# Linear attention and a two-layer feed-forward: one hand-fixed order of 3436 operations replaced by another

## The chip, the cores and the metric

The kernel runs on one core of a Trainium2 chip. The metric is the device time of one execution in microseconds (us): the median of three runs is 794.76 us before the change, with 792.8 and 801.1 as the lowest and the highest. The core has a matmul engine (PE, with its weight loads shown apart as PEld), three engines for elementwise work (DVE, ACT, POOL) and the queue engine SP, which issues most DMAs; ACT issues some. Each engine takes its instructions strictly in the order in which the program lists them, and an instruction that must wait holds up all that stand behind it on its engine.

## The reference

```
q_s = exp(q - max(q over d));  q_s /= sum(q_s over d) + 1e-9
k_s = exp(k - max(k over s));  k_s /= sum(k_s over s) + 1e-9
kv  = einsum("bhsd,bhse->bhde", k_s, v)
x   = einsum("bhsd,bhde->bhse", q_s, kv)     # 8 batches, 8 heads, 576 rows, 64 wide
x   -> 4608 tokens x 512
h   = x @ w_in                               # 512 x 2048
g   = h if h >= 1; 0 if h <= -1; else (h + 1)^2 / 4
out = g @ w_out                              # 2048 x 512
```

## The kernel before, in words

The 4608 tokens are cut into 9 chunks of 512. Per chunk the attention is done for pairs of heads: softmax of q and k on DVE, ACT and POOL, the products k^T v (`kv`, line 1288, for the first chunk line 1044) and q times kv (`x`, line 918) on PE. All large matmuls work on pairs of rounded numbers: a value is stored as a high part (a CAST on ACT) and the rest (a subtraction on DVE or POOL), and each product is three matmuls, high by low, high by high and low by high. The weights arrive as 64-bit numbers (`st`, loads of 512 KB) and are taken apart in the first chunk: ACT scales (`sg`, line 579), DVE shifts and joins (lines 584 and 587), ACT rounds to the high part (line 610), POOL subtracts (line 614). The parts of w_in go to a buffer in DRAM (`b`) and are fetched again (`w`, line 652) for later chunks.

Chunks 0 to 2 are computed plainly. For a block f of 128 of the 2048 hidden units, the first layer fills one PSUM bank (`h`, line 1499, 12 matmuls of 512 columns), ACT and POOL or ACT build the squared ramp (`r`, lines 1669 and 1673 or 1675), DVE clips it into the bank (line 1679), ACT rounds it (`g`, line 1721), DVE subtracts (line 1725), and the second layer adds it to four output banks (`o`, line 1736). The bank of block f is free for block f + 3 once the subtraction of line 1725 is done. Chunks 3 to 8 go in pairs by a scheme of seven block products in place of eight: the first layer with `hA`, `hb`, `hC` (line 1563), its sums on DVE (line 1587), the same ramp (now into rooms called B11, B12, B21, B22), sums of these rooms (line 1841), their rounding on ACT (line 1855) and the subtraction on DVE or POOL (line 1859), then the second layer (`yA`, `yB`, `yC`, line 1879). The bank of the last `hA` of a pair is also the first `yB` bank.

The maxima of k that the softmax subtracts travel through DRAM: DVE finds and turns them (`kmax`, `mt`, lines 1245 and 1251), SP stores them (`mk`, line 1255) and loads them back to all 128 partitions (`m`, line 1263), and DVE subtracts them from k (line 1272).

Nothing is scheduled at run time. A planner builds 3436 operations with their dependences; the tuple `SEQUENCE` holds the numbers of all of them in the order in which they are emitted, and each engine gets its share of that order. An operation that can be done by two engines has a second way, and the tuple `SECOND` lists the operations that take it (427 of them): most are subtractions and sums that DVE does in place of POOL, some are copies that DVE does in place of ACT. `Plan.settle` applies both tuples; buffers that rotate are assigned in the order of the sequence too.

Of the kernel before, what the change touches and what calls it, by code (L numbers as in the profile page):

```python
# [99 lines left out]
class Ring:  # L100
# [31 lines left out]
    1, 43, 20, 0, 19, 44, 95, 62, 11, 2, 46, 63, 12, 102, 30, 13, 21, 31, 47, 86, 14, 87, 128,  # L132
    88, 3, 89, 45, 15, 90, 4, 22, 91, 16, 92, 32, 54, 93, 64, 94, 23, 33, 55, 17, 330, 34, 96,
    25, 331, 18, 65, 35, 6, 56, 109, 24, 97, 26, 36, 57, 7, 37, 98, 27, 58, 49, 99, 5, 59, 8,
    66, 48, 9, 104, 100, 103, 28, 73, 50, 10, 105, 51, 74, 29, 68, 106, 67, 38, 107, 75, 69, 76,
    52, 70, 130, 154, 129, 77, 135, 60, 41, 131, 78, 39, 71, 61, 53, 132, 40, 79, 72, 133, 332,
    115, 80, 333, 81, 180, 42, 334, 310, 111, 134, 141, 156, 155, 101, 335, 82, 142, 336, 312,
    157, 84, 83, 167, 110, 337, 85, 168, 158, 112, 338, 169, 159, 137, 113, 170, 136, 116, 114,
    171, 138, 117, 339, 182, 143, 181, 172, 161, 311, 139, 118, 183, 318, 140, 193, 119, 173,
    194, 184, 340, 187, 120, 144, 185, 206, 174, 121, 195, 175, 196, 122, 232, 145, 123, 219,  # L140
    162, 163, 146, 220, 197, 164, 124, 165, 147, 126, 341, 166, 148, 221, 342, 149, 222, 189,
    213, 188, 127, 313, 343, 322, 198, 152, 190, 321, 178, 344, 191, 208, 125, 207, 314, 192,
    223, 209, 151, 224, 199, 153, 345, 239, 210, 234, 316, 150, 315, 200, 211, 176, 214, 201,
    177, 215, 346, 258, 179, 216, 203, 225, 233, 317, 347, 245, 217, 319, 235, 226, 246, 479,
    218, 227, 236, 205, 241, 240, 247, 237, 265, 242, 248, 260, 202, 284, 249, 323, 228, 259,
    243, 229, 261, 250, 231, 244, 262, 251, 271, 320, 252, 263, 291, 272, 724, 253, 273, 324,
    267, 266, 274, 349, 204, 268, 275, 286, 254, 269, 276, 285, 230, 270, 287, 297, 277, 298,
    288, 293, 356, 292, 299, 289, 325, 294, 255, 348, 295, 300, 375, 278, 296, 326, 301, 279,
    302, 382, 256, 327, 458, 329, 460, 328, 282, 351, 350, 478, 257, 352, 362, 303, 353, 363,
    358, 357, 354, 364, 304, 359, 365, 305, 360, 406, 281, 377, 290, 376, 361, 283, 378, 388,  # L150
    384, 383, 459, 379, 389, 385, 469, 366, 390, 380, 413, 461, 367, 309, 462, 386, 480, 391,
    463, 466, 368, 401, 392, 464, 481, 432, 369, 393, 280, 402, 370, 482, 308, 387, 403, 307,
    483, 408, 419, 420, 407, 470, 485, 394, 409, 395, 484, 415, 410, 414, 416, 396, 487, 465,
    404, 439, 417, 373, 411, 486, 433, 306, 421, 422, 471, 371, 434, 445, 446, 447, 423, 435,
    436, 374, 440, 437, 424, 468, 448, 418, 372, 467, 472, 400, 397, 497, 398, 488, 441, 442,
    449, 473, 425, 443, 426, 489, 399, 474, 427, 490, 510, 511, 450, 451, 512, 381, 491, 186,
    452, 475, 499, 430, 429, 444, 513, 428, 492, 493, 477, 494, 523, 504, 476, 498, 453, 500,
    501, 431, 506, 609, 505, 1306, 507, 496, 514, 607, 457, 502, 525, 524, 526, 530, 456, 531,
    527, 238, 554, 515, 528, 454, 536, 1394, 455, 508, 537, 538, 495, 509, 532, 533, 405, 627,
    539, 516, 517, 608, 549, 518, 519, 520, 534, 628, 567, 556, 629, 550, 552, 553, 568, 521,  # L160
    540, 541, 503, 569, 685, 705, 551, 561, 630, 535, 555, 610, 611, 557, 558, 542, 543, 706,
    707, 631, 544, 570, 562, 571, 563, 564, 559, 708, 580, 545, 632, 581, 572, 686, 944, 565,
    586, 573, 612, 587, 582, 588, 613, 589, 574, 522, 590, 575, 546, 633, 438, 634, 615, 745,
    614, 583, 584, 746, 566, 747, 687, 616, 709, 617, 264, 725, 591, 547, 529, 748, 592, 593,
    646, 710, 648, 594, 711, 647, 548, 712, 692, 635, 693, 694, 585, 688, 689, 691, 713, 690,
    721, 649, 695, 578, 718, 637, 636, 1172, 638, 722, 597, 639, 560, 577, 749, 696, 719, 731,
    618, 750, 732, 697, 108, 576, 733, 771, 734, 579, 596, 941, 698, 595, 699, 946, 620, 778,
    650, 723, 779, 943, 601, 598, 599, 780, 781, 651, 737, 735, 619, 600, 700, 758, 736, 621,
    738, 741, 759, 652, 772, 640, 701, 751, 702, 641, 642, 643, 760, 742, 773, 782, 720, 603,
    703, 752, 753, 602, 605, 774, 761, 762, 657, 763, 622, 714, 715, 645, 791, 644, 775, 716,  # L170
    623, 777, 704, 864, 792, 783, 764, 740, 765, 654, 810, 667, 793, 653, 784, 794, 776, 807,
    766, 666, 804, 862, 756, 624, 658, 668, 669, 817, 795, 769, 743, 805, 818, 717, 656, 670,
    730, 671, 757, 808, 673, 819, 1487, 820, 822, 770, 739, 809, 785, 754, 726, 831, 832, 786,
    844, 845, 672, 796, 821, 833, 863, 865, 744, 755, 797, 798, 626, 660, 866, 834, 835, 1073,
    836, 846, 847, 811, 901, 674, 659, 661, 867, 823, 873, 940, 848, 799, 902, 675, 625, 655,
    903, 767, 768, 908, 909, 868, 827, 789, 837, 870, 788, 662, 824, 676, 677, 678, 1303, 874,
    787, 910, 606, 663, 679, 828, 911, 849, 850, 838, 904, 800, 1130, 905, 806, 869, 826, 1076,
    680, 907, 790, 802, 664, 934, 935, 851, 803, 665, 825, 912, 839, 842, 160, 852, 682, 684,
    857, 829, 681, 921, 860, 906, 861, 913, 914, 922, 872, 801, 915, 923, 916, 875, 843, 871,
    1301, 683, 882, 936, 937, 924, 947, 858, 876, 925, 840, 987, 926, 830, 948, 938, 961, 949,  # L180
    962, 963, 841, 974, 951, 927, 855, 975, 950, 883, 964, 212, 953, 952, 954, 1483, 877, 976,
    957, 988, 928, 1132, 989, 859, 878, 1026, 814, 977, 958, 939, 853, 856, 978, 884, 929, 1028,
    604, 995, 990, 959, 979, 980, 885, 919, 854, 920, 965, 917, 886, 887, 918, 991, 992, 1397,
    879, 1065, 1066, 993, 955, 994, 930, 996, 997, 960, 998, 889, 966, 981, 1176, 1173, 1392,
    967, 1027, 1035, 956, 931, 968, 969, 891, 982, 999, 1067, 1029, 1079, 933, 1030, 1008, 888,
    1000, 1001, 1009, 1068, 1010, 1011, 890, 1038, 1071, 1170, 932, 1080, 1002, 892, 971, 984,
    1069, 1081, 1072, 893, 894, 972, 1082, 1003, 1083, 895, 896, 1093, 1085, 1094, 1095, 1032,
    973, 986, 1084, 1037, 1096, 898, 1131, 1106, 1133, 1086, 1070, 881, 1031, 970, 1034, 1074,
    1087, 1012, 1013, 1033, 1089, 1014, 900, 1097, 1005, 880, 1098, 897, 899, 729, 983, 1107,
    1108, 1109, 1090, 1091, 1004, 1015, 1016, 985, 1021, 1046, 1047, 816, 1110, 1099, 1177,  # L190
    1006, 1036, 1040, 1178, 1017, 1141, 1100, 1088, 1179, 1180, 1048, 1049, 1101, 1134, 1022,
    1023, 1217, 1183, 1092, 1218, 1039, 1184, 1007, 1186, 1050, 1181, 1051, 1024, 1018, 1185,
    1020, 1111, 1103, 1112, 1052, 1053, 1041, 1138, 1113, 1105, 1054, 1102, 1055, 1019, 1169,
    1042, 1056, 1057, 1139, 1114, 1182, 1204, 1078, 1205, 1225, 1116, 1115, 1058, 1206, 1219,
    1187, 1059, 1135, 1226, 1136, 1060, 1061, 1188, 1137, 1119, 1025, 1043, 727, 1063, 1044,
    1104, 1117, 1207, 1150, 1045, 1127, 1142, 1227, 1143, 1228, 1208, 1220, 1221, 1222, 1209,
    1129, 1191, 1192, 1193, 1194, 1579, 1140, 1189, 1210, 1062, 1128, 1121, 1229, 1230, 1145,
    1118, 1144, 1211, 1299, 1231, 1064, 1658, 1195, 1196, 1146, 1122, 1151, 1212, 1197, 1305,
    1232, 1190, 1120, 1152, 1223, 1198, 1300, 1321, 1293, 1294, 1322, 1323, 1256, 1125, 1254,
    1199, 1324, 1325, 1224, 1307, 1126, 1238, 1296, 355, 1147, 1201, 1577, 1297, 1298, 1239,  # L200
    1233, 1123, 1655, 1153, 1326, 1327, 1203, 1154, 1155, 1156, 1240, 1200, 1157, 1213, 1334,
    1255, 412, 1241, 1242, 1148, 1347, 1348, 1308, 1309, 1158, 1216, 1257, 1258, 1259, 1243,
    1244, 1335, 1214, 1237, 1160, 1159, 1161, 1310, 1260, 1202, 1215, 1328, 1236, 1149, 1162,
    1245, 1163, 1164, 1336, 1246, 1265, 1311, 1262, 1313, 1165, 1337, 1266, 1338, 1171, 1312,
# [2059 lines left out]
```

## Time and profile before

| | us |
|---|---|
| median of 3 runs (lowest, highest) | 794.76 (792.8, 801.1) |
| span of the profiled execution, first to last instruction | 791.4 |
| PE busy with matmuls | 780.8 |
| DVE busy | 610.0 |
| ACT busy | 469.3 |
| POOL busy | 395.5 |

The span is that of one profiled execution; what lies around it (start and end of the program) isn't in the trace, and the profiled execution has no time of its own beside the span. The median of the runs is 3.4 us above the span. Busy times are sums of instruction durations without overlap; matmuls are pipelined, so that two neighbours overlap and their number times their duration is more than the busy time.

### The profile page before, as it was taken

The numbers are of one execution on the slowest core, as the hardware profiler recorded it, in microseconds if no ns is written. First come the engines' busy times: TensorE is split into PE (matmuls) and PEld (weight loads), VectorE is DVE, ScalarE is ACT, GpSimd is POOL, SyncE is SP. The second block draws the span as 40 slices with busy tenths as digits, with TensorE's granted clock in tenths as the row PEclk, the third lists the DMA queues.
The fourth block names the chain that finished last, engine by engine and source line by source line (L and its number), as shares of the span: only waits on it lengthen the run. The fifth ranks groups of instructions, "written<-read, shape, count | busy, mean of one in ns | idle before, by whom it ended". The sixth has DMA issues, their size and how long they took to land.

```text
span 791.4 us, 12315 instructions
## 1 busy us (share of the span) xinstructions
PE 780.8 (99%) x4136; PEld 630.1 (80%) x4136; DVE 610.0 (77%) x1035; ACT 469.3 (59%) x868; POOL 395.5 (50%) x343
## 2 busy tenths in 40 slices
PE   8999999999999999999999999999999999999998
PEld 6777878877777778877778888777778888888886
DVE  7988887667788888788789886887797846669843
ACT  7868775555565665655675664665756625555560
POOL 5766466745456556356653465346405632344250
PEclk9999999999999999999999999999999999999999
DMA  8988998999799787987777767756656746667663
GB/s 315 294 269 287 298 338 276 319 311 363 263 336 320 258 304 233 348 302 251 228 221 256 233 245 249 248 185 212 192 180 222 245 163 207 204 187 231 211 207 136
DMA packets 76462, 200.74 MB, mean 254 GB/s; under 512 B 8688, under 2 KB 16880, under 8 KB 76400
## 3 DMA queue, kind: packets, MB, share of 16 engines
q1 hardware_dynamic: 64160, 174.43, 66.0%
q10 hardware_dynamic: 12240, 25.54, 10.1%
q8 instruction: 33, 0.54, 0.3%
q14 instruction: 29, 0.24, 0.1%
HBM read 159.02 MB, written 40.91 MB: 253 GB/s over the span
## 4 chain that ended last, share of the span: by engine, by line
PE 86%; DVE 4%; DMA 4%; ACT 3%; issue 1%; POOL 1%; SPq 0%; POOLq 0%; DVEq 0%; ACTq 0%
PE hA L1563 16%; PE yA L1879 16%; PE o L1736 13%; PE h L1499 12%; PE yC L1879 8%; PE hC L1563 8%; PE yB L1879 4%; PE hb L1563 4%; PE kv L1288 2%; PE x L918 2%; DMA st<-in_w 1%; DMA kt<-in_kt 1%; DVE st L587 1%; DMA w<-b 1%; DMA m<-mk 1%
## 5 line engine op out<-in xcount | busy, mean ns | idle before, releaser
L1855 ACT CAST y<-B 128x512 fp32r<-128x512 f32 x160 | 99.0, 621 | 79.3 <-PE yA L1879 34.9
L1563 PE MATMUL hA<-x,w 128*128 128x512 f32 x576 | 142.5, 390 | 0.0
L1859 POOL TENSOR_TENSOR y<-B,y 128x512 fp32r<-128x512 f32 x55 | 74.3, 1356 | 113.7 <-ACT y L1855 104.1
L1563 PEld LDWEIGHTS hA<-x,w 128*128 128x128 f32 x576 | 107.8, 188 | 23.2 <-DVE sn_P L481 0.8
L1879 PE MATMUL yA<-y,w_y 128*128 128x512 f32 x528 | 124.5, 390 | 0.0
L1736 PE MATMUL o<-wh,g 128*128 128x512 f32 x384 | 118.6, 390 | 0.0
L1879 PEld LDWEIGHTS yA<-y,w_y 128*128 128x128 f32 x528 | 98.9, 188 | 21.4 <-ACT y L1855 0.8
L1499 PE MATMUL h<-x,w 128*128 128x512 f32 x432 | 109.5, 392 | 0.8 <-DVE g L1725 0.8
L1859 DVE TENSOR_TENSOR y<-B,y 128x512 fp32r<-128x512 f32 x105 | 83.7, 802 | 32.5 <-ACT y L1855 31.8
L1675 POOL TENSOR_TENSOR r<-r 128x512 f32<-128x512 f32 x46 | 50.5, 1102 | 94.6 <-ACT r L1669 89.5
L1499 PEld LDWEIGHTS h<-x,w 128*128 128x128 f32 x432 | 80.4, 188 | 19.1 <-DVE g L1725 1.8
L1736 PEld LDWEIGHTS o<-wh,g 128*128 128x128 f32 x384 | 72.1, 188 | 15.2 <-DVE g L1725 0.6
L1736 PE MATMUL o<-wl,g 128*128 128x512 f32 x192 | 76.0, 396 | 0.6 <-ACT g L1721 0.6
L1563 PE MATMUL hC<-x,w 128*128 128x512 f32 x288 | 73.3, 392 | 0.0
L1879 PE MATMUL yC<-y,w_y 128*128 128x512 f32 x288 | 66.7, 389 | 0.0
L1673 ACT ACTIVATE r<-r 128x512 f32<-128x512 f32 x98 | 61.3, 630 | 5.7 <-DMA r<-wh 2.4
L1563 PEld LDWEIGHTS hC<-x,w 128*128 128x128 f32 x288 | 53.7, 188 | 11.8 <-ACT sn_P L479 0.3
L1879 PEld LDWEIGHTS yC<-y,w_y 128*128 128x128 f32 x288 | 54.1, 188 | 11.2
L1841 DVE TENSOR_TENSOR B<-B,B 128x512 f32<-128x512 f32 x72 | 51.7, 735 | 0.6
L1396 POOL TENSOR_TENSOR q<-q,qmb 128x512 f32<-128x512 f32 x32 | 36.0, 1138 | 30.2 <-DVE qmb L1388 21.7
L1396 POOL TENSOR_TENSOR q<-q,qzb 128x512 f32<-128x512 f32 x32 | 35.4, 1118 | 26.5 <-DVE qzb L1418 17.8
L1736 PEld LDWEIGHTS o<-wl,g 128*128 128x128 f32 x192 | 36.0, 188 | 11.8 <-issue 3.5
(156 smaller groups left out, 1404.5 us busy)
## 6 DMA issues: line engine op xcount, KB each, us to landing
w_y<-r SPq DMA_DIRECT2D x84, 512.0 KB, 4.1
w<-b SPq DMA_DIRECT2D x50, 512.0 KB, 5.5
w<-s SPq DMA_DIRECT2D x48, 512.0 KB, 4.6
st<-in_w SPq DMA_DIRECT2D x32, 512.0 KB, 6.2
s<-w_s SPq DMA_DIRECT2D x16, 512.0 KB, 6.1
r<-w_o SPq DMA_DIRECT2D x32, 256.0 KB, 4.8
v<-in_v ACTq DMA_DIRECT2D x20, 325.0 KB, 4.7
k<-in_k ACTq DMA_DIRECT2D x20, 320.0 KB, 5.1
```

The lines of the kernel that those rows point to most:

```text
L918: nc.tensor.matmul(flat(r)[cols, p0:p1], kvt[rows, g % NKV, pr, :], q[pr]["tq"].rearrange("p j t -> p (j t)")[rows, p0:p1], start=True, st ...
L1288: nc.tensor.matmul(kv[d, i, :], t[pr]["k"][:, j, d], t[pr]["v"][:, j, e * (D + 1) : (e + 1) * (D + 1)], start=(j == 0), stop=(j == KJ - 1) ...
L1396: nc.gpsimd.tensor_tensor(qf, qf, at, alu)
L1499: nc.tensor.matmul(t["h"], lhs, rhs, start=(turn == 0 and i == 0), stop=(turn == NPAIR - 1 and i == 2),)
L1563: nc.tensor.matmul(banks[b]["h"], lhs, rhs, start=(begins and not kk and not m), stop=(ends and kk == 1 and m == 2), skip_group_check=True,)
L1673: nc.scalar.activation(t["r"], t["r"], AF.Square)
L1675: nc.gpsimd.tensor_tensor(t["r"], t["r"], t["r"], ALU.mult)
L1736: nc.tensor.matmul(outs[c, j], lhs[:, s], rhs, start=(begins and i == 0), stop=(closes and i == 2),)
L1841: eng.tensor_tensor(gr[p, to], gr[p, a], gr[p, b], alu)
L1855: nc.scalar.copy(t["gh"], gr[p, PART_ROOM[part]])
L1859: eng.tensor_tensor(t["gl"], gr[p, PART_ROOM[part]], f32(t["gh"]), ALU.subtract)
L1879: nc.tensor.matmul(banks[b, i], lhs, rhs, start=(begins and not m), stop=(ends and m == 2), skip_group_check=True,)
```

## The change

Only the two tuples change. `SEQUENCE` has the same 3436 numbers in another order: an operation stands on average 8.5 places from where it stood, the largest moves are 165 places ahead and 176 back, and the 200 places from 1800 on are the same. `SECOND` has 440 numbers in place of 427. DVE has 1053 instructions in place of 1035, ACT (its DMA issues included) 947 in place of 949, POOL 323 in place of 339; PE has the same matmuls. The longer tuple moves every later line down by one, so that line 1679 of before is line 1680 of the changed kernel.

```
 SEQUENCE = (
-    1, 43, 20, 0, 19, 44, 95, 62, 11, 2, 46, 63, 12, 102, 30, 13, 21, 31, 47, 86, 14, 87, 128,
...
 SECOND = (
-    10, 27, 29, 51, 61, 70, 72, 146, 172, 198, 276, 328, 329, 393, 450, 476, 491, 605, 625, 626,
...
```

**SP, first chunk, about 40 us into the program.** The names: `k_1_1` is a load of k of chunk 1, `st5_1` and `st7_0` are weight loads, `mk1_0` the store of the maxima, `m2_1_0` their load back. Before:

```order
L1235 DMA v_1_1_693<-in_v 128x650
L1235 DMA k_1_1_700<-in_k 128x640
L572 DMA st5_1_730<-in_w 128x1024
L1255 DMA mk1_0_189<-mt_1_0_715 4x32 x2
L572 DMA st7_0_754<-in_w 128x1024
L1263 DMA m2_1_0_766<-mk1_0_189 128x256
L1235 DMA v_1_0_775<-in_v 128x650
```

Now:

```order
L573 DMA st4_1_690<-in_w 128x1024
L1236 DMA k_1_0_721<-in_k 128x640
L1256 DMA mk1_0_189<-mt_1_0_708 4x32 x2
L1236 DMA v_1_1_738<-in_v 128x650
L573 DMA st5_1_743<-in_w 128x1024
L1264 DMA m2_1_0_760<-mk1_0_189 128x256
L573 DMA st7_0_765<-in_w 128x1024
```

The store of the maxima stood behind the weight load st5_1 and now stands ahead of it; the load back stood behind the weight load st7_0 and now stands ahead of it, and st5_1 is behind one more load of v.

**DVE, chunk 1, about 180 us into the program.** The names: `sw_6`, `ss_6`, `w_s_6`, `os_5` and `w_o_5` are sums of weights for the later chunks, `h_1_10` is the bank of block 10 of chunk 1 that line 1679 clips, `kmax`, `qa`, `qmo`, `qmb`, `z` and `rz` belong to the softmax. Before:

```order
L684 TENSOR_TENSOR sw_6_2177<-w_1_13_2171 128x512
L1679 SCALAR_TENSOR_TENSOR h_1_11_2141<-h_1_11_2141,r_1_11_2215 128x512
L1370 TENSOR_REDUCE qa_3_0_2217<-q_3_1_2154 128x16
L1388 TENSOR_TENSOR qmb_3_0_2251<-qa_3_0_2217,qmo_3_0_2246 128x32
L698 TENSOR_TENSOR ss_6_2256<-ss_6_2256,sw_6_2177 128x256
L1299 TENSOR_SCALAR z_3_0_2260<-kv_3_0_2180 128x2
L1301 RECIPROCAL rz_3_0_2262<-z_3_0_2260 128x2
L736 TENSOR_TENSOR w_s_6_0_2264<-ss_6_2256,w_s_6_0_2264 128x2x256
L698 TENSOR_TENSOR ss_6_2256<-sw_6_2177 128x256
L698 TENSOR_TENSOR ss_6_2256<-sw_6_2177,ss_6_2256 128x256
L1679 SCALAR_TENSOR_TENSOR h_1_10_2126<-h_1_10_2126,r_1_10_2241 128x512
L1245 TENSOR_REDUCE kmax_94<-kt_4_0_2201 128x1
```

Now:

```order
L1680 SCALAR_TENSOR_TENSOR h_1_9_2026<-h_1_9_2026,r_1_9_2157 128x512
L941 TENSOR_TENSOR x10_2106<-x_2_0_0_2057,x10_2106 128x512
L787 TENSOR_TENSOR os_5_2115<-ow_5_2054 128x256
L1680 SCALAR_TENSOR_TENSOR h_1_10_2131<-h_1_10_2131,r_1_10_2180 128x512
L685 TENSOR_TENSOR sw_6_2217<-w_1_12_2183 128x512
L832 TENSOR_TENSOR w_o_5_1_2189<-os_5_2115,w_o_5_1_2189 128x2x256
L1726 TENSOR_TENSOR g_1_9_2226<-h_1_9_2026,g_1_9_2226 128x512
L1300 TENSOR_SCALAR z_3_0_2253<-kv_3_0_2194 128x2
L1302 RECIPROCAL rz_3_0_2255<-z_3_0_2253 128x2
L699 TENSOR_TENSOR ss_6_2232<-ss_6_2232,sw_6_2217 128x256
L1246 TENSOR_REDUCE kmax_94<-kt_4_0_2242 128x1
L1680 SCALAR_TENSOR_TENSOR h_1_11_2172<-h_1_11_2172,r_1_11_2250 128x512
```

The clip of h_1_10 stood ten rows behind the first sum sw_6 and right behind two sums ss_6; now it stands ahead of the sums of group 6 that DVE does, with the subtraction of x10 and one sum os_5 just ahead of it.

**ACT, chunks 5 and 6, about 565 us into the program.** The names: `r_5_15` is the ramp of the last hA bank of that pair (its first row is the ramp, line 1669, its second the square, line 1673), `y_5_1_0` to `y_5_1_2` are roundings for the second layer. Before:

```order
L1855 CAST y_5_0_7_6329<-B11_5_7_6327 128x512
L1669 ACTIVATE r_5_15_6331<-hA_5_7_6120,half_93 128x512
L1855 CAST y_5_1_0_6345<-B21_5_0_5619 128x512
L1855 CAST y_5_1_1_6353<-B21_5_1_5717 128x512
L1673 ACTIVATE r_5_15_6331<-r_5_15_6331 128x512
L1181 CAST x10_6360<-xw_8_0_5968 128x512
L1855 CAST y_5_1_2_6370<-B21_5_2_5857 128x512
```

Now:

```order
L1856 CAST y_5_0_7_6343<-B11_5_7_6330 128x512
L1856 CAST y_5_1_0_6347<-B21_5_0_5668 128x512
L1670 ACTIVATE r_5_15_6349<-hA_5_7_6111,half_93 128x512
L1674 ACTIVATE r_5_15_6349<-r_5_15_6349 128x512
L1856 CAST y_5_1_1_6367<-B21_5_1_5717 128x512
L1856 CAST y_5_1_2_6377<-B21_5_2_5898 128x512
```

Two roundings stood between the ramp of r_5_15 and its square; now none does, and one of the two stands ahead of the ramp.

## Rows read from the trace of the kernel before

**Rows 1.** Part 1 of the page, each engine: busy us, share, instructions.

```profile
PE 780.8 (99%) x4136; PEld 630.1 (80%) x4136; DVE 610.0 (77%) x1035; ACT 469.3 (59%) x868; POOL 395.5 (50%) x343
```

**Rows 2.** Stretches: from:to, length, then PE, PEld, DVE, ACT, POOL busy, clock, DMA.

```profile
0.00:21.00 21.00, 17.41 (x160) 13.69 (x160) 15.56 (x41) 15.10 (x32) 11.92 (x18) 1.00 0.88 312
54.00:62.00 8.00, 6.50 (x39) 4.55 (x39) 7.43 (x11) 6.62 (x11) 5.56 (x4) 1.00 0.71 240
62.00:184.00 122.00, 121.81 (x728) 97.63 (x724) 90.52 (x172) 78.57 (x152) 73.23 (x66) 1.00 0.92 313
184.00:188.00 4.00, 3.42 (x16) 2.48 (x15) 3.91 (x8) 2.83 (x6) 3.26 (x3) 1.00 0.97 315
188.00:566.00 378.00, 378.00 (x2086) 304.46 (x2085) 310.26 (x539) 225.01 (x425) 199.92 (x175) 1.00 0.78 261
566.00:570.00 4.00, 2.98 (x13) 2.17 (x12) 4.00 (x8) 3.57 (x7) 0.00 (x0) 1.00 0.78 225
570.00:787.60 217.60, 217.60 (x963) 179.08 (x961) 150.26 (x215) 112.25 (x189) 78.94 (x60) 1.00 0.63 201
787.60:791.40 3.80, 0.08 (x1) 0.00 (x0) 0.00 (x0) 0.58 (x1) 0.00 (x0) 1.00 0.20 69
```

**Rows 3.** What PE waited for: us in total, times, longest.

```profile
PE yB L1879 <- DVE B L1679: 1.0, 1, 1.0
...
PE kv L1288 <- DVE st L587: 0.9, 1, 0.9
...
PE h L1499 <- DVE g L1725: 0.8, 2, 0.6
...
PE o L1736 <- ACT g L1721: 0.6, 1, 0.6
```

**Rows 4.** Timeline 41 to 62 us: start, length, engine, line, operation [idle before].

```profile
41.05 0.20 DVE L1251 STREAM_TRANSPOSE mt<-kmax 128x32 f32<-128x32 f32 x1
...
42.50 0.33 SPq L572 DMA_DIRECT2D st<-in_w  x1
...
42.92 1.15 SPq L1255 DMA_DIRECT2D mk<-mt  x2
...
46.31 0.33 SPq L1263 DMA_DIRECT2D m<-mk  x1
...
52.57 0.83 DVE L1272 TENSOR_TENSOR k<-k,m 128x640 f32<-128x640 f32 x1 [2.16 <-DMA st<-in_w]
...
54.03 0.65 ACT L610 CAST x<-st 128x512 fp32r<-128x512 f32 x1 [2.44 <-DVE st L587]
```

**Rows 5.** DMA issues by line: KB each, median us to landing.

```profile
m<-mk SPq DMA_DIRECT2D x14, 128.0 KB, 6.2
```

**Rows 6.** Timeline 179 to 187 us.

```profile
179.06 0.69 DVE L684 TENSOR_TENSOR sw<-w 128x512 f32<-128x512 f32 x1 [4.27 <-DMA w<-b]
...
183.00 0.63 ACT L1673 ACTIVATE r<-r 128x512 f32<-128x512 f32 x1
...
183.82 0.41 DVE L698 TENSOR_TENSOR ss<-sw 128x256 f32<-128x256 f32 x1
...
184.49 0.69 DVE L1679 SCALAR_TENSOR_TENSOR h<-h,r 128x512 f32<-128x512 f32 x1
```

**Rows 7.** Timeline 565 to 569 us.

```profile
565.07 0.69 ACT L1669 ACTIVATE r<-hA,half 128x512 f32<-128x512 f32 x1
...
565.65 1.16 ACT L1855 CAST y<-B 128x512 fp32r<-128x512 f32 x2
...
567.79 0.68 DVE L1679 SCALAR_TENSOR_TENSOR B<-hA,r 128x512 f32<-128x512 f32 x1
```

**Rows 8.** Timeline of the end.

```profile
779.36 8.32 PE L1879 MATMUL yA<-x,w_y 128*128 128x512 f32 x36
```

**Rows 9.** Line 1859 by engine: ns min/median/max, first to last start.

```profile
L1859 DVE TENSOR_TENSOR y<-B,y x105: 650/692/1770, 395.1 to 774.8; 128x512 fp32r<-128x512 f32 x105
...
L1859 POOL TENSOR_TENSOR y<-B,y x55: 1282/1294/1826, 327.5 to 769.5; 128x512 fp32r<-128x512 f32 x55
```

491 rows, old and new, of tables (SECOND, SEQUENCE) are left out of this document.

## The prediction

> **What bounds the kernel now.** I read part 1 of the page first: PE is busy for 780.8 of 791.4 us, the next engine, DVE, for 610.0 [rows 1]. A busy share over the span says nothing of single stretches, so the second view is the table of stretches [rows 2]. In it PE is busy without a break for 378.00 us from 188 us and for 217.60 us from 570 us. All idle time of PE lies in six of the stretches: 3.59 us in the first 21 us (21.00 less 17.41), 1.50 from 54 us, 0.19 from 62 us, 0.58 from 184 us, 1.02 from 566 us, and 3.72 at the end, where the last output is copied and stored. In the body, between 21 and 787.6 us, PE loses 3.29 us in all. The granted clock is 1.00 in each stretch, the upper of the two levels, 2.4 GHz.
>
> The list of waits names the five pauses of the body [rows 3]: `o` waits 0.6 us for a rounding on ACT, `kv` 0.9 us for a join of weights on DVE, `h` twice, 0.6 and 0.2, for a subtraction on DVE, and `yB` 1.0 us for a clip on DVE. In the three stretches with long pauses DVE is busy for 7.43 of 8, 3.91 of 4 and 4.00 of 4 us [rows 2]: PE waits there for a queue of work on DVE, in which the wanted operation stands too far back. That is what an order can mend, and where another order can do harm.
>
> **The change, term by term.** PE's matmuls are the same in number, so what it can win is idle time, and what it can lose is new idle time.
>
> *SP at 40 us, two pauses.* The maxima are turned by 41.25 us (start 41.05, length 0.20) [rows 4]. Their store is issued at 42.92, since the weight load ahead of it goes out at 42.50. The load back goes out at 46.31 and takes 6.2 us to land [rows 5], that is until 52.5; DVE's subtraction from k begins at 52.57 after 2.16 us of idle time. The profile names a weight load as what ended that idle time, but the landing of the maxima falls on it to 0.1 us, and I take this as the cause. Behind that subtraction stand the join and the clip, ACT's cast of weights starts at 54.03 after 2.44 us of idle time [rows 4], `o` comes 0.6 late and, through the same weights, `kv` 0.9 late. Now the store stands ahead of the weight load: it can leave at about 41.3, 1.6 us sooner (42.92 less 41.3), and the load back stands ahead of the next weight load. What is late next is the weight load st5_1, which waits behind the store pair (1.15 us) and a load of v; its block is needed on PE only some blocks later. 1.6 us sooner covers 0.6 and then 0.9 us (the second only if the weights gain the same), so I take -1.5 us. Bounds: 0, if the load back is held up elsewhere on SP, and -1.5.
>
> *DVE at 180 us.* The clip of bank h_1_10 begins at 184.49 though its square ended on ACT at 183.63 (183.00 and 0.63); two sums of weights stand in between, the first from 183.82 [rows 6]. They in turn go back to the sum that begins at 179.06 after DVE waited 4.27 us for a DMA. In the new order the clip is ahead of that sum, and could begin by 183.82 or earlier: 0.67 sooner. The pause there is 0.58 [rows 2]; the gain just covers it, and I take -0.5. Bounds 0 and -0.6.
>
> *ACT at 565 us.* Ramp at 565.07, two casts from 565.65 (1.16 us together), then the square, then the clip at 567.79 [rows 7]. Now one cast stands ahead of the ramp and none between: the ramp moves 0.53 later (half of 1.16, less the overlap), and the square comes 0.58 after it, at 566.2 in place of 566.7; with one sum fewer ahead of it on DVE the clip can begin at about 567.2. That is 0.6 us off a pause of 1.0: I take -0.6. Bounds 0 and -1.0.
>
> *The head.* PE has 3.59 us of idle time in 21 us; the order of loads is nearly the same, that of transposes and softmax steps is not. Nothing in the rows says what the new order needs there. Bounds: -3.6, all idle time, and +1.3, one subtraction on POOL (1294 ns in the median [rows 9], the nearest row for an operation put ahead of a wanted one). I take 0, between them.
>
> *Other picks.* DVE has 18 instructions more, POOL 16 fewer, ACT 2 fewer. The largest group of them is line 1859, 692 ns on DVE and 1294 on POOL in the median [rows 9]. 18 by 0.69 is 12.4 us more on DVE. From 570 us DVE is busy for 150.26 of 217.60 us, from 188 us for 310.26 of 378.00 [rows 2]; idle time of 67 us in each covers them, so they cost nothing, unless they fall in stretches like those of the pauses.
>
> The two engines don't leave each other alone: the longest of line 1859 is 1770 ns on DVE and 1826 on POOL, against least times of 650 and 1282 [rows 9]. The Trainium skill, page "SBUF — State Buffer", section "Who interferes with whom", states that a DVE instruction with two SBUF inputs and a GpSimd instruction that reads SBUF exclude each other for the whole instruction, and whoever starts second blocks. By that rule, with which the maxima agree, each added instruction could cost DVE a wait of up to one POOL operation besides its own time, 18 by 1.29 or 23 us more, still inside the idle time above.
>
> *New pauses.* PE's groups stand in another order, and any of them may now find its operand late. The only measure is this trace: five pauses in 766 us, the shortest 0.2. I add 0.2; the bounds are 0 and 3.3, a full new set.
>
> *Sum:* -1.5 - 0.5 - 0.6 + 0 + 0.2 = -2.4 us on the span of 791.4, thus 789.0. The runs' median is 794.76, 3.4 above the span; the same on top gives **792.4 us**.
>
> **The rivals.**
>
> *A: gains are spent.* The pauses go, and others of their size come where operations moved back. For it: the pauses are short, and 3400 operations moved. Against it: two stretches of hundreds of microseconds hold without a pause. Time: 794.8 to 798.1 (a new set of 3.3 and no gain).
>
> *B: DVE becomes the bound.* The instructions taken over from POOL land where PE already waits for DVE. For it: DVE is full in all three long pauses [rows 2]. Against it: the idle time of 67 us in the two long stretches. Each that lands there pushes the wanted clip back by 0.69; from 12 of the 18 on the loss is over 8 us. All 18: 794.8 + 12.4 = 807.2, and none of the gains.
>
> *C: all idle time of body and head goes:* 794.8 - 3.3 - 3.6 = 787.9. Against it: the head waits for loads and for a softmax chain that has to run in any order.
>
> *D: the pace of PE changes.* A busy PE need not be PE at its best. At the end 36 matmuls take 8.32 us [rows 8], 0.231 us each; in the 217.60 us from 570 us there are 963 matmuls [rows 2], 0.226 each. If the pace hung on which groups follow each other, a reordering could gain without a pause to remove: the 2% between these readings are 15 us of the body's 766, which would give 779. Against it: the first reading holds the last matmul's whole length, and PE runs at one pace through first and second layers alike. The Trainium skill, page "TensorE: Matmul & The Clock Gate", section "Wait — 56ns, not 53.3ns?", gives 215.7 ns from start to start at 512 columns on a warm array. The trace is slower than that in both readings; by the page's figure, as an estimate, the body would be 5% or some 36 us shorter.
>
> That the change does nothing at all can be left out: the three places read above differ in the program.
>
> **The numbers.** Forecast (790 to 794.5) 0.60, A 0.24, B 0.07, C 0.07, D 0.02. From no change one can tell about 1% here, 8 us: faster than 786.8 or slower than 802.7. Faster: D and the far end of C, 0.03. Slower: B, 0.07. The rest, 0.90, is within 1%. The range is 788.5 to 798: its lower end takes in the sum with the lower bounds of the three places and half of the head's, its upper end is that of A; B, D and part of C stay outside.
>
> **What would show it.** The store of the maxima within 0.5 us of their turning, and no idle time of DVE over 1 us ahead of the first subtraction of line 1272 (now 1273): the SP term. No wait of `h` for line 1725 (now 1726) near 185 us: the DVE term. `yB` waiting less than 0.5 us near 565 us: the ACT term. PE idle outside head and end below 1.5 us: no new set; above 3.3 us A holds, and with DVE full at each of its pauses B. A pace of PE below 0.22 us per matmul in a stretch without waits would be D. The forecast is wrong in mechanism if the time falls while the five pauses stand, and in size if the head moves by more than 1 us.

## The result and the profile after

The new order is slower. The median of 20 runs is 798.89 us (793.97 to 804.45), that of the kernel before, run beside it 20 times, 793.37 us (791.76 to 801.10); the ratio is 1.0063, with a 95% interval from 1.0044 to 1.0082. Ratios here and below are formed from the single runs and differ a little from the quotient of two medians (here 1.0070), and one run of 2013.27 us in e12 is left out of its ratio. The forecast was 792.4 us in a range from 788.5 to 798.0: wrong in sign, and the time lies 0.9 us outside the range. The 794.76 us that the forecast started from, a median of three, was itself 1.4 us above the median of 20. Each run on record took 1.7 to 2.2 us longer than its own span, so the 3.4 us that the prediction put on top of the span were too much by about that 1.4.

The head of the page after and the table of stretches, cut as in [rows 2] with 21 to 54 us added (columns: stretch, its length, then busy us and instructions of PE, PEld, DVE, ACT, POOL, then the granted clock, the share of DMA and GB/s):

```profile
span 797.1 us, 12302 instructions
...
PE 781.4 (98%) x4136; PEld 627.9 (79%) x4136; DVE 611.1 (77%) x1053; ACT 468.7 (59%) x866; POOL 376.0 (47%) x327
```

```profile
0.00:21.00 21.00, 16.71 (x171) 13.18 (x171) 15.88 (x42) 16.39 (x36) 13.09 (x18) 1.00 0.92 328
21.00:54.00 33.00, 32.21 (x143) 25.00 (x136) 27.40 (x49) 27.17 (x52) 20.28 (x17) 1.00 0.85 273
54.00:62.00 8.00, 8.00 (x70) 6.53 (x69) 5.94 (x13) 6.68 (x12) 5.53 (x5) 1.00 0.88 300
62.00:184.00 122.00, 118.79 (x682) 93.75 (x681) 98.60 (x180) 72.97 (x137) 69.63 (x62) 1.00 0.89 305
184.00:188.00 4.00, 4.00 (x19) 3.34 (x18) 2.88 (x5) 2.23 (x5) 2.20 (x3) 1.00 0.91 238
188.00:566.00 378.00, 374.39 (x2061) 299.18 (x2061) 306.20 (x540) 220.87 (x417) 191.07 (x165) 1.00 0.79 258
566.00:570.00 4.00, 4.00 (x20) 3.30 (x19) 3.50 (x7) 2.49 (x8) 2.14 (x4) 1.00 0.86 265
570.00:787.60 217.60, 217.60 (x964) 179.18 (x963) 149.96 (x222) 119.31 (x203) 72.07 (x57) 1.00 0.65 206
```

Against [rows 1, 2]: PE's busy time is the same to 0.6 us and the clock stands at 1.00, so of the 5.7 us that the span grew by 5.1 are idle time of PE. Between 21 and 787.6 us PE now loses 0.79 + 3.21 + 3.61 = 7.61 us, where it lost 3.29. The three short stretches that held the pauses of before (54, 184 and 566 us) are full. Of the 7.61 us, 7.37 lie between 40 and 250 us; from 250 us to 787.6 us PE loses nothing. The list of PE's waits, which answers to [rows 3], with the small ones and those of the head left out (columns: who waited <- for whom, total us, times, longest):

```profile
PE x L919 <- DVE st L588: 1.5, 2, 0.9
PE o L1737 <- DVE g L1726: 1.4, 1, 1.4
PE kv L1289 <- ACT r L1670: 1.4, 1, 1.4
...
PE h L1500 <- DMA w<-b: 1.3, 2, 0.8
PE h L1500 <- DVE g L1726: 0.9, 1, 0.9
...
PE h L1500 <- DVE x L941: 0.5, 2, 0.3
```

PE falls idle ahead of these matmuls at 70.8 and 100.4 us (`x`), 86.6 (`kv`), 192.5 and 236.9 (`h` for a load of w), 226.0 (`h` for g) and 246.6 us (`o`).

### The profile page after: what moved, and what is told of

The parts are those of the page before. It is cut to its first block, busy times and chain, and to the rows that moved or that the text cites. A ratio compares the mean times of both kernels' runs of the same rounds, so it can differ in the third digit from the quotient of the medians.

```text
span 797.1 us, 12302 instructions
## 1 busy us (share of the span) xinstructions
PE 781.4 (98%) x4136; PEld 627.9 (79%) x4136; DVE 611.1 (77%) x1053; ACT 468.7 (59%) x866; POOL 376.0 (47%) x327
## 3 DMA queue, kind: packets, MB, share of 16 engines
q10 hardware_dynamic: 12240, 25.54, 10.1%
## 4 chain that ended last, share of the span: by engine, by line
PE 68%; ACT 0%; issue 0%; DVE 0%
PE hA L1564 17%; PE yA L1880 17%; PE hC L1564 8%; PE yC L1880 8%; PE o L1737 5%; PE yB L1880 4%; PE hb L1564 4%; PE h L1500 3%; PE x L919 1%; PE kv L1289 1%; ACT yo L480 0%; DVE os L787 0%
## 5 line engine op out<-in xcount | busy, mean ns | idle before, releaser
L1500 PE MATMUL h<-x,w 128*128 128x512 f32 x432 | 113.3, 393 | 2.6 <-DMA w<-b 1.3
L1860 POOL TENSOR_TENSOR y<-B,y 128x512 fp32r<-128x512 f32 x47 | 63.4, 1353 | 111.3 <-ACT y L1856 111.1
L1860 DVE TENSOR_TENSOR y<-B,y 128x512 fp32r<-128x512 f32 x113 | 85.7, 762 | 36.0 <-ACT y L1856 34.9
L1676 POOL TENSOR_TENSOR r<-r 128x512 f32<-128x512 f32 x45 | 48.3, 1075 | 100.7 <-ACT r L1670 96.1
L1397 POOL TENSOR_TENSOR q<-q,qmb 128x512 f32<-128x512 f32 x32 | 38.5, 1217 | 37.8 <-DVE qmb L1389 31.6
L1670 ACT ACTIVATE r<-h,half 128x512 f32<-128x512 f32 x48 | 32.8, 688 | 32.4 <-PE h L1500 32.3
```

Source lines behind the costliest of these rows:

```text
L1397: nc.gpsimd.tensor_tensor(qf, qf, at, alu)
L1500: nc.tensor.matmul(t["h"], lhs, rhs, start=(turn == 0 and i == 0), stop=(turn == NPAIR - 1 and i == 2),)
L1670: nc.scalar.activation(t["r"], t["h"], AF.Relu, bias=half[:, :1], scale=0.5)
L1676: nc.gpsimd.tensor_tensor(t["r"], t["r"], t["r"], ALU.mult)
L1860: eng.tensor_tensor(t["gl"], gr[p, PART_ROOM[part]], f32(t["gh"]), ALU.subtract)
```

## The experiments

A number of the sequence is called a place. Only certain places can be cut: those up to which both orders hold the same operations (384, 420, 620, 1282, 1500, 2310 are such). On the clock they lie near 72, 79, 117, 240, 288 and 468 us. In the diffs SEQUENCE_BEFORE is the table of before. Where places are exchanged, SECOND is split the same way; where single operations are moved, after's picks stay. The changed picks are not spread evenly: of the 175 operations whose pick differs, 3 stand in the places 384 to 620, 58 in 620 to 1282 and 68 from 2310 on. Each profile is that of one execution. Ratios are to the kernel before, run on the same chip, with a 95% interval.

### Where the loss is made

**One stretch, the picks, the head.**

```
e1   +SEQUENCE = SEQUENCE[:420] + SEQUENCE_BEFORE[420:1500] + SEQUENCE[1500:]
e2   +SECOND = SECOND_BEFORE
e3   +SEQUENCE = SEQUENCE[:420] + SEQUENCE_BEFORE[420:]
e4   e3, and  +SEQUENCE = [n for n in SEQUENCE if n != 290];  SEQUENCE.insert(360, 290)
```

> After, but places 420 to 1500 of the order (some 79 to 288 us of the program) and their picks are those of before; the first 420 places and all from 1500 on stay those of after. Theory Q (the new pauses of TensorE between 70 and 250 us come from transfers and operations that were moved within these places on the queues of SP, ScalarE and VectorE): the 6 us that TensorE loses there against before are gone and the gains of the other places stay, 790.5 to 793.0 us. Theory P (the changed picks make VectorE late all over the program, the order matters little): about half of the changed picks are outside the stretch, so about half of the loss stays, 795 to 797 us.

Measured: 795.29 us, ratio 1.0021 (0.9997 to 1.0046), runs from 790.81 to 800.87. The median lies in theory P's range and above Q's, and the interval reaches from there down to just above Q's: too wide to decide. In its profile the pauses that Q names are gone (0.80 us idle from 62 to 188 us and 0.10 from 188 to 260, where after loses 3.21 and 3.61), but 2.05 us stand between 260 and 300.

> After's order, with before's choice of engine wherever two engines can do an operation. Theory Q (the order of the queues): the loss stays, 797 to 800 us. Theory P (18 more instructions on VectorE make it late at the pauses): the loss goes, 791 to 794 us.

Measured: 805.03 us, 1.0144 (1.0122 to 1.0166). Theory P falls, and Q's number was wrong too: the new order is 6 us slower with the old picks than with its own. The new picks belong to the new order.

> Before, with after's order and picks in the first 420 places (the first 79 us) alone. In the profile of after TensorE is 1.9 us ahead of before at 66 us and only 0.3 us ahead at 86 us, though the order of the places 384 to 455 is the same in both. Theory S (the store of b8, 512 KB, which was moved 36 places forward on SP's queue ahead of the loads of st10, st9, kt and q, makes those loads land late and eats the lead): 793.0 +- 0.4 us, since that store is moved here too. Theory R (the transfers run at their own pace in this stretch, so that no lead can be kept, store or no store): 793.0 +- 0.4 us too. Theory of the prediction (the lead is kept to the end): 791.5 us.

Measured: 792.81 us, 1.0002 (0.9980 to 1.0023).

> As the run with after's first 420 places alone, but the store of b8 is put back at before's place, behind the load of st11. Theory S (the moved store eats the lead): the lead is kept, 791.5 +- 0.5 us. Theory R (the pace of the transfers eats it): 793.0 +- 0.4 us, no better than with the store moved.

Measured: 793.53 us, 0.9996 (0.9977 to 1.0015). Moving the store of b8 back gives nothing that can be told; theory S has no support, though the interval (from 791.6 us) still touches its range. The lead that the head has at 66 us is not in the time at the end in either.

**The tail alone, and the places 384 to 620.**

```
e6   +SEQUENCE = SEQUENCE[:384] + SEQUENCE_BEFORE[384:620] + SEQUENCE[620:]
e8   +SEQUENCE = SEQUENCE_BEFORE[:2310] + SEQUENCE[2310:]
```

> After, with the places 384 to 620 (some 72 to 117 us) and their picks as before. In after, VectorE runs operations of the attention (the low part of x5, two transposes) ahead of the join of st13, and the decoding of the weights st13 to st15 is 2.4 to 3.6 us later than in before. Theory D (that order makes the pauses at 86, 100, 106 and 110 us): TensorE loses no more than 1.5 us between 70 and 125 us where it lost 4.2, 795.5 to 797 us. Theory R (the transfers set this stretch): no gain, 798 to 800 us.

Measured: 796.17 us, 1.0038 (1.0022 to 1.0054), against 1.0063 with the stretch as in after. The time is in theory D's range, but the two intervals overlap, so this run alone doesn't show a gain.

> Before, with after's order and picks from place 2310 on (from some 468 us). The third term of the prediction alone: the wait of yB for VectorE's B near 565 us goes, and nothing comes in its place. 792.2 us (1.2 us less, the wait's whole gap in the row of matmuls). If the time is given back before the end: 793.4 us.

Measured: 793.08 us, 0.9988 (0.9977 to 0.9999): the third gain of the prediction is there, and the interval just leaves out no change (by the medians it is 0.5 us). What else this run shows is told below.

**Each half of the suspected stretch alone, both undone, and head and tail together.**

```
e9   +SEQUENCE = SEQUENCE_BEFORE[:384] + SEQUENCE[384:620] + SEQUENCE_BEFORE[620:]
e10  +SEQUENCE = SEQUENCE_BEFORE[:620] + SEQUENCE[620:1282] + SEQUENCE_BEFORE[1282:]
e11  +SEQUENCE = SEQUENCE[:384] + SEQUENCE_BEFORE[384:1282] + SEQUENCE[1282:]
e12  +SEQUENCE = SEQUENCE[:420] + SEQUENCE_BEFORE[420:2310] + SEQUENCE[2310:]
```

> Before, with after's order and picks in the places 384 to 620 alone (some 72 to 117 us). Theory D (the order of the decoding against the attention in these places costs what undoing it in after gave back, 0.3 to 0.4 %): 795.5 to 797 us, with new waits of TensorE between 80 and 115 us. Theory R (these places cost nothing by themselves, only behind after's head): 793 to 794 us.

Measured: 796.23 us, 1.0028 (1.0012 to 1.0045), in theory D's range.

> Before, with after's order and picks in the places 620 to 1282 alone (some 117 to 240 us). Theory D2 (the rest of the loss, 0.38 % after the places 384 to 620 were undone, is made here: in every profile that has after's order here, TensorE loses 2.2 to 2.6 us between the matmuls 1200 and 1300): 795.5 to 797 us. Theory X (the rest is made behind place 1282): 793 to 794 us.

Measured: 798.12 us, 1.0064 (1.0043 to 1.0084): theory X falls, and the stretch costs more by itself than D2 expected.

> After, with the places 384 to 1282 and their picks as before. Theory D + D2 (all of the loss is in these places; head and tail keep their small gains): 792 to 793.5 us. Theory X (places behind 1282 cost as well): 795 to 796 us.

Measured: 793.71 us, 1.0000 (0.9981 to 1.0019), 0.2 us above the range of D + D2 and well below X's.

> Before, with after's places 0 to 420 and from 2310 on. If the two gains add up (0.6 us measured for the head alone, not told from nothing, and 0.5 us for the tail alone): 792.2 to 792.6 us. If the lead of the head is spent on the way: 793.0 us, the tail's gain alone.

Measured: 792.90 us, 1.0002 (0.9975 to 1.0029): no better than before. No version that beats both kernels by more than e8's 0.1% came out of this.

The times settle the place: put into the kernel before, each half costs by itself, and with both undone the loss is gone. (The halves alone add up to 0.92%, the whole loss is 0.63%; the intervals allow both readings, so it isn't shown that the costs add.) The first 71 of the places 384 to 620 are the same in both orders, so that the first half of the loss comes from the places behind these.

The profiles bear out the second half only. The stretches of before and after (from:to, length, then PE's busy time first):

```profile
62.00:125.00 63.00, 62.80 (x359) 50.17 (x355) 53.04 (x99) 47.17 (x90) 37.10 (x32) 1.00 0.94 319
...
188.00:260.00 72.00, 72.00 (x450) 57.42 (x449) 57.61 (x109) 41.41 (x86) 41.01 (x39) 1.00 0.90 315
```

```profile
62.00:125.00 63.00, 59.79 (x313) 46.43 (x312) 50.77 (x87) 42.64 (x83) 36.49 (x30) 1.00 0.86 288
...
188.00:260.00 72.00, 68.39 (x396) 52.85 (x397) 55.12 (x107) 35.98 (x72) 37.42 (x35) 1.00 0.87 292
```

In e9, after's order at 384 to 620:

```profile
62.00:125.00 63.00, 61.13 (x323) 48.50 (x323) 52.03 (x97) 44.41 (x86) 36.93 (x32) 1.00 0.90 307
...
188.00:260.00 72.00, 72.00 (x450) 57.44 (x449) 57.21 (x108) 40.53 (x85) 39.99 (x37) 1.00 0.93 324
...
566.00:600.00 34.00, 32.98 (x149) 26.06 (x148) 29.27 (x48) 21.50 (x38) 2.67 (x3) 1.00 0.59 190
```

In e10, after's order at 620 to 1282:

```profile
62.00:125.00 63.00, 61.63 (x326) 49.24 (x326) 52.84 (x93) 46.81 (x89) 36.67 (x32) 1.00 0.91 311
...
188.00:260.00 72.00, 70.40 (x438) 54.87 (x437) 53.30 (x107) 38.07 (x76) 40.54 (x39) 1.00 0.89 301
```

In e11, after's order everywhere but there:

```profile
62.00:125.00 63.00, 61.12 (x322) 48.20 (x321) 52.73 (x96) 45.13 (x87) 35.36 (x30) 1.00 0.91 310
...
188.00:260.00 72.00, 72.00 (x451) 57.38 (x450) 60.20 (x117) 40.67 (x84) 38.46 (x36) 1.00 0.90 310
...
566.00:600.00 34.00, 34.00 (x155) 27.22 (x154) 31.62 (x50) 22.32 (x40) 2.76 (x3) 1.00 0.63 195
```

From 188 to 260 us PE loses 3.61 us in after and 1.60 in e10, where the order there is after's, and nothing in before, e9 and e11, where it is before's. All 20 profiles agree: 0 to 0.92 us in the eight with before's order at 620 to 1282, 1.60 to 6.44 us in the twelve with after's or with after's in part. From 566 us PE loses 1.02 us with before's tail and nothing with after's. From 62 to 125 us one profile tells nothing: e9 loses 1.87 us, but so does e11 with before's order there (1.88), and e10 loses 1.37. Over all profiles it is 0.20 to 2.08 us with before's order at 384 to 620 (eleven, 1.1 in the mean) and 0.35 to 3.21 with after's (seven, 2.1 in the mean, the mixed e13 and e14 left out). So the cost of the first half rests on the time of e9, and on that of e6 as far as it goes. What e9 shares with after is the pause of `kv`, 1.4 us for line 1670:

```profile
PE kv L1289 <- ACT r L1670: 1.4, 1, 1.4
...
PE kv L1289 <- DVE st L588: 1.2, 1, 1.2
PE yB L1880 <- DVE B L1680: 1.0, 1, 1.0
```

It stands at 0.8 to 1.5 us in six of those seven profiles, and at 0.4 to 0.8 us in three of the eleven with before's order.

### By what it is made: single waits

At 86 us one can see how such a wait arises. In before, PE does the matmuls of `o` by wl9 (three, 0.7 us) ahead of `kv` and comes to `kv` at 87.5 us; what it needs is there at 87.24, the end of the second exponential of k. In after that group of `o` stands 20 places further back, PE is through at 86.6, and ScalarE, which has taken both exponentials of k ahead of line 1670, ends that at 87.72. One group less stands ahead of `kv`, and what `kv` needs comes 0.5 us later. First before, then after:

```profile
86.52 0.72 ACT L1278 ACTIVATE k<-k 128x640 f32<-128x640 f32 x1
...
87.47 1.21 PE L1288 MATMUL kv<-v,k 128*64 128x65 f32 x34
```

```profile
85.78 1.36 ACT L1279 ACTIVATE k<-k 128x640 f32<-128x640 f32 x2
...
87.04 0.68 ACT L1670 ACTIVATE r<-h,half 128x512 f32<-128x512 f32 x1
...
87.94 0.77 PE L1289 MATMUL kv<-v,k 128*64 128x65 f32 x19 [1.36 <-ACT r L1670]
```

At 226 us it is ScalarE's queue. The timeline of after (ACTq: a load is issued from ScalarE's queue):

```profile
222.34 1.80 ACTq L1236 DMA_DIRECT2D kt<-in_kt  x1
...
224.23 0.77 ACTq L1236 DMA_DIRECT2D v<-in_v  x1
...
225.04 0.50 ACTq L1236 DMA_DIRECT2D kt<-in_kt  x1
...
225.59 1.07 ACT L1722 CAST g<-h 128x512 fp32r<-128x512 f32 x2 [2.68 <-DMA out<-osb]
...
226.21 0.69 DVE L1726 TENSOR_TENSOR g<-h,g 128x512 fp32r<-128x512 f32 x1 [2.29 <-ACT g L1722]
```

Three issues hold the queue from 222.34 to 225.54; the cast behind them, then the subtraction on DVE, then PE wait. The engines are not busy there: from 224 to 227 us DVE works for 0.79 us of 3.00 and ACT for 1.41. In before the same loads of kt go out from 219 to 229 us (two of them 0.46 us apart), and each issue takes a third of a microsecond (ns, least/median/most; before, then after):

```profile
L1235 ACTq DMA_DIRECT2D kt<-in_kt x4: 334/335/363, 219.4 to 229.2; - x4
```

```profile
L1236 ACTq DMA_DIRECT2D kt<-in_kt x4: 353/776/1797, 222.3 to 232.4; - x4
```

At 246 us it is a late load. DVE stands for 5.21 us and takes the clip and the subtraction, for which PE waits, behind the maximum:

```profile
241.60 0.75 DVE L1246 TENSOR_REDUCE kmax<-kt 128x1 f32<-128x576 f32 x1 [5.21 <-DMA kt<-in_kt]
...
243.97 0.67 DVE L1680 SCALAR_TENSOR_TENSOR h<-h,r 128x512 f32<-128x512 f32 x1
...
247.32 0.63 DVE L1726 TENSOR_TENSOR g<-h,g 128x512 fp32r<-128x512 f32 x1
```

That kt goes into a buffer that the `kv` matmul of chunk 3 frees. In before this matmul starts at 224.3 us, in after at 230.6, and its v was issued at 221 and 224 us in place of 211 and 218. Five loads were moved to take this away, alone and with the places 384 to 620 undone:

```
e5   +MOVES = ((1139, 1218), (1142, 1139), (1300, 1122), (1256, 1190), (1254, 1256))   # (operation, put behind)
e7   e6's line, and the same MOVES
```

> After, with five loads moved forward and nothing else: v_3_2 and v_3_3 (they stand 42 and 18 places behind before's, and the kv matmul of chunk 3 waits for them), kt_4_3 and kt_4_2 (into the two buffers that this matmul frees) and w_2_5 (behind two sums that took its buffer of the weight ring, so that it waits until the last matmul of w_2_4). Theory L (these loads, by the turn in which the rings hand out buffers, make the pauses of after at 225.6, 236.6 and 246.2 us): the pauses at 236 and 246 us go, 2.5 us or more, 795.0 to 796.6 us. Theory E (the loads are late because the engines in front of them are late, and moving them gives nothing): 798 to 800 us.

Measured: 799.36 us, 1.0078 (1.0055 to 1.0100), no better than after. The pauses at 226 and 246 us are not in its profile (the one profile here whose granted clock stood at 0.95 throughout), but one of 1.6 us at 234 is, and others at 189 and 289 us.

> Both edits together: places 384 to 620 as before, and the five loads moved forward. Theories D and L add up: 792.0 to 794.5 us, as before. If the two stretches hang together (a gain in the first is paid back in the second), no better than the better of the two alone, 795 us or more.

Measured: 796.75 us, 1.0054 (1.0035 to 1.0072), no better than e6. Theory L falls: the waits moved, the time stayed.

### By what it is made: one side of the order

```
e13  +SEQUENCE = SEQUENCE[:384] + WINDOW + SEQUENCE[620:]      # PE's operations in before's order
e14  the same; SP, DVE, ACT and POOL in before's order, PE in after's, after's picks
e15  +SEQUENCE = SEQUENCE[:620] + WINDOW + SEQUENCE[1282:]     # PE's operations in before's order
```

> After, with TensorE's matmuls alone in before's order within the places 384 to 620; the other queues keep after's order. Theory M (TensorE has used up its filling work early: the matmuls of o_0_2 by wl9 stand behind the kv matmul and not ahead of it, so it asks 0.7 us sooner for what is not there yet): 795.5 to 796.8 us, as with the whole stretch undone. Theory F (the feeding queues, with x5 and two transposes ahead of the join of st13, deliver late): 798 to 800 us. Theory T (the orders of the engines belong together, and half a change is worse than a whole one): 800 us or more.

Measured: 801.63 us, 1.0088 (1.0064 to 1.0113).

> The complement: after, with SP, VectorE, ScalarE and GpSimd in before's order within the places 384 to 620, and TensorE's matmuls in after's. Theory M: 798 to 800 us. Theory F: 795.5 to 796.8 us. Theory T: 800 us or more.

Measured: 799.75 us, 1.0074 (1.0051 to 1.0098).

> After, with TensorE's matmuls alone in before's order within the places 620 to 1282, the stretch that costs 0.64 % by itself. Theory M: 794.5 to 796 us. Theory F: 798 to 800 us. Theory T: 800 us or more.

Measured: 807.96 us, 1.0186 (1.0166 to 1.0205). In its list of waits one takes 3.6 us, for ScalarE's copy of `x` out of PSUM, which in this mixed order comes late for the matmul that wants the bank:

```profile
PE h L1500 <- ACT xw L480: 3.6, 1, 3.6
PE h L1500 <- DMA w<-b: 2.8, 2, 1.9
```

M falls by e13 and e15, F by e14: with one side put back the time is that of after (e14, 0.3 us short of T's number) or worse, with both sides better (e11, and e6 as far as it can be told). Half a change costs as much as the whole or more, as in e2. The other half of e15, the places 620 to 1282 with the feeding engines alone in before's order, was not run. A limit of these three: the operations of the engines had to be interleaved anew, and buffers that rotate may be handed out in another turn than in either kernel.

### By what it is made: the named waits once more

```
e16  +MOVES = ((1577, 1296), (1579, 1577))
e17  +MOVES = ((1577, 1296), (1579, 1577), (1300, 1122))
e18  e6's line, and e17's MOVES
```

> After, with ScalarE's issues of the loads kt_5_0 and kt_5_1 put where before has the first, behind the two casts of g and the relu that they stood ahead of. In every profile with after's order here ScalarE stands in these issues for 2 to 3 us at 220 to 225 us, and the cast of g_2_1 behind them ends 1 us late for TensorE. Theory I (the issues hold the queue): the pause near 225 us goes, 1.0 to 1.5 us less, 797.2 to 798 us. Theory J (the cast would find another wait): 798.5 to 799.5 us, and a pause of 0.8 us or more between 215 and 230 us.

Measured: 797.39 us, 1.0048 (1.0032 to 1.0064); the time is in theory I's range, but against after's 1.0063 the intervals overlap. The loads of kt are issued in 0.36 and 0.47 us at 226 us, and the pause at 226 is gone. But the issues that stand in their spot now take long (v 1.49 us), and PE waits 2.1 us for a load of w at 233 us:

```profile
218.18 1.03 ACTq L1236 DMA_DIRECT2D q<-in_q  x1
...
219.49 1.49 ACTq L1236 DMA_DIRECT2D v<-in_v  x1
...
225.91 0.36 ACTq L1236 DMA_DIRECT2D kt<-in_kt  x1
```

```profile
PE h L1500 <- DMA w<-b: 2.8, 2, 2.1
```

> After, with the two load issues of ScalarE put behind the casts, and the load of w_2_5 put ahead of the stores of osb on SP's queue and ahead of the two sums that take its buffer of the weight ring. With the issues alone moved (797.4 us), TensorE stands 2.1 us at 233 us for w_2_5, which goes out 0.3 us behind the store of osb_1_3. Theory I + L (each of the two is a wait of its own): that pause goes too, 795.0 to 796.4 us. Theory T (the queues are paced together; a wait taken away here comes back a few microseconds later): 797 to 798.5 us.

Measured: 797.30 us, 1.0050 (1.0032 to 1.0069). From 215 to 260 us PE now waits twice, 0.9 and 1.2 us:

```profile
PE o L1737 <- DVE g L1726: 1.2, 1, 1.2
PE h L1500 <- DMA w<-b: 0.9, 1, 0.9
```

> The same three moves, and the places 384 to 620 with their picks as before. Theory I + L + D (the named places carry most of the loss): 792.8 to 794.3 us. Theory T (only the whole stretch, undone together, brings the time back): 795 to 796.5 us, no better than the places 384 to 620 alone (796.2 us).

Measured: 796.34 us, 1.0037 (1.0020 to 1.0054), as e6 alone. The times of e17 and e18 lie in theory T's range: a named wait can be taken away, and the time stays within what can be told.

## Why the prediction was wrong, point by point

- **What bounds the kernel.** PE, with idle time as the only thing to win or lose: right, and 5.1 of the 5.7 us by which the span grew are idle time.
- **SP at 40 us, -1.5.** The mechanism came as described. The maxima are turned by 40.47 us, their store goes out at 40.50, the subtraction from k starts at 49.48 where it was 52.57, and the stretch from 54 us is full. Rows of after:

```profile
40.27 0.20 DVE L1252 STREAM_TRANSPOSE mt<-kmax 128x32 f32<-128x32 f32 x1
...
40.50 1.15 SPq L1256 DMA_DIRECT2D mk<-mt  x2
...
49.48 1.38 DVE L1273 TENSOR_TENSOR k<-k,m 128x640 f32<-128x640 f32 x1
```

  The size failed, and for a reason that no view of one trace shows: the pauses at 54 and 60 us don't come with the order of before in every execution. e8 has that order up to place 2310, and its profile has no pause from 21 to 62 us, where before loses 1.50 [rows 2]; e9 and e10, with the same first 384 places, lose 1.23 and 0.96. With after's first 384 places PE loses 0 to 2.12 us there, and in e6, e14 and e16 `kv` waits again for the join, 1.2 to 1.3 us; the mean is 0.56 us over sixteen profiles, against 0.92 over the four with before's. In turn e8 stands 2.3 us near 290 us, where before, by the same order, stands not at all. Rows of e8:

```profile
21.00:62.00 41.00, 41.00 (x217) 32.71 (x217) 36.08 (x65) 33.88 (x63) 29.98 (x24) 1.00 0.87 286
...
260.00:566.00 306.00, 303.70 (x1623) 244.06 (x1622) 252.67 (x428) 183.72 (x343) 156.72 (x132) 1.00 0.74 244
566.00:600.00 34.00, 34.00 (x154) 27.26 (x153) 31.62 (x51) 22.31 (x40) 2.63 (x3) 1.00 0.62 196
```

  The head alone (e3, e4) gives nothing that can be told from no change.
- **DVE at 180 us, -0.5.** The stretch from 184 us is full, as forecast, and this holds beyond one profile: from 180 to 192 us PE loses 0.13 to 1.15 us in each of the eight with before's order there, and nothing in eight of the twelve with after's. It lies inside the places 620 to 1282, which as a whole cost 0.64%.
- **ACT at 565 us, -0.6.** Right, and larger: the whole pause of 1.0 us went in every profile with after's tail and in none with before's, and e8 measures 0.12% for it (0.01 to 0.23; 0.06% by the medians), where 1.0 us would be 0.13%. With after's order and the old picks (e2) 0.6 us of it is back: order and picks are needed together.
- **The head, 0.** It lost 0.70 us in this profile (16.71 us busy for 17.41), inside its bounds. PE is idle there for 3.26 to 3.59 us in the four profiles with before's first 384 places and for 3.11 to 5.13 in the sixteen with after's (4.2 in the mean).
- **Other picks, 0.** DVE's busy time rose by 1.1 us (611.1 for 610.0), not by the 12.4 taken as the most. The 18 are a net number: 94 operations take their second way that didn't, and 81 no longer do. B as a rival falls: of the places where PE waits, DVE is nearly full at 84 to 88 us (3.73 of 4.00) and 241 to 248 (6.19 of 7.00), but not at 99 to 102 (1.79 of 3.00), 224 to 227 (0.79) and 235 to 238 (1.39), and without the new picks the new order is slower still (e2). By the Trainium skill, page "SBUF — State Buffer", section "Who interferes with whom", a DVE instruction with two SBUF inputs and a GpSimd instruction that reads SBUF exclude each other; the prediction's estimate by it was up to 23 us on top. The sums of the row do not show it.
- **New pauses, +0.2, bounds 0 and 3.3. This is the step that failed.** It measured 7.61 us: that is the idle time of the body, and none of it stands at the old places. The old pauses gave back their 3.29 us in this profile, and the head lost 0.70; with 0.1 at the end that makes the 5.1 us. The prediction counted the pauses of before, five in 766 us, and took their number as the rate at which any order of 3436 operations would meet them. The runs show that it is no such rate: after's order loses 3.61 us from 188 to 260 us, where before has no pause at all, and e2, e13, e14 and e15, which mix the two orders or their picks, are 0.7 to 1.9% slower than before. That the old order had been fitted as a whole to what these places need is the likely reading, but it is argued. The argument against rival A, that two stretches of hundreds of microseconds hold without a pause, took for a property of the work what the old order had reached: in after 3.61 us are lost in the first of them, all ahead of 250 us. Where the new pauses are, transfers are dense: a DMA share of 0.89 from 62 to 184 us, against 0.65 from 570 us, where there are none. But before has 0.92 from 62 to 184 us and loses 0.19 there [rows 2], so density alone makes no pause; that little room in the transfers is where an order matters is not tested.
- **Rival A, 794.8 to 798.1 at 0.24,** is the case that came, past its own upper end, because that end allowed one new set of pauses and no more.
- **The range.** By the terms named for it (1.5, 0.6, 1.0 and half of 3.6 off 794.8) its lower end comes to 789.9, not 788.5; the measured time lies beyond the other end.
- **D.** PE's pace did not change: 964 matmuls in the 217.60 us from 570 us, 0.226 us each, as before.

Open: which of the moves within the places 384 to 1282 cost what, and why. The five runs that moved single loads and issues (e5, e7, e16 to e18) moved the pauses and not, or hardly, the time; the one run that clearly gave it back (e11) undid the whole stretch, both sides together.

## What to carry to other kernels

A pause that one profile shows may be absent when the same part of a program runs again: before a gain is priced by it, look at a second trace, or at another kernel that shares that part. When one full order replaces another, the few pauses that the old trace still has are no rate for the new one (here 3.29 us became 7.61): leave the upper bound at two or three times as much. And undo or transplant whole stretches, at places where both orders have done the same work, before hunting single waits: that found where the loss is made, while moving the waits named in the trace did not give it back.

## What the runs showed of the hardware that was not expected

- A load's issue on ScalarE's queue takes 0.33 us in the median in both kernels, at most 0.80 in before and up to 1.80 us in after (the kt at 222 us), and holds what stands behind it: the cast that follows three issues starts at 225.59, when they end at 225.54. It is not bound to the load: moved away (e16), kt takes 0.36 us and the v that stands in its spot 1.49 us, but in e17, with the same two moves, that v takes 0.33. Nor does it come with after's order alone: in e8 a kt takes 1.71 us at 254 us, in a part that e8 has in common with before, where it takes 0.36. What holds it was not tried. The Trainium skill, page "DMA: Bandwidth & Descriptors", section "Issuing engines are not separate DMA queues", says that issuing from several engines saves only the time to initiate a DMA, usually small against the DMA itself; here three issues, 3.2 us with the gaps between them, were long enough to stop the matmuls for 0.9 us.
- The same 2310 places of the same order gave pauses of 1.7 and 0.6 us near 290 us in one execution (e8) and none in another (before), at a granted clock of 1.00 in both.
- The runs of after spread over 10.5 us (793.97 to 804.45), those of before beside them over 9.3 (791.76 to 801.10) and those of e1 over 10.1 (790.81 to 800.87): more than the 5.5 us that the change was worth, so that a median of three runs says little here. What makes the spread was not tried.
